# One-core cross-attention and SwiGLU kernel: float64 weights converted in pieces of 1024, exponent bounds on ScalarE, attention one batch ahead

## The chip, the core and the metric

The kernel runs on one NeuronCore of a Trainium2 chip. The engines are named as the profile names them: PE (TensorE, matmuls; PEld its weight loads), DVE (VectorE), ACT (ScalarE), POOL (GpSimd) and SP (SyncE, which here only issues DMAs). The metric is the device time of one execution in microseconds (us), lower is better. Each engine takes its instructions in the order in which the program has them and waits at an instruction until what that one needs is there.

## The reference

Inputs are float32 but for the three weight matrices, which arrive as float64: `x` [8, 8, 512, 64], `state` [8, 8, 32, 64], `w_gate` and `w_val` [512, 1536], `w_out` [1536, 512], `rms_g` [512].

```
# attention, for each batch and head
scores  = scale * x @ state.T;   a  = softmax(scores);   xread = a @ state     # 512 rows
scores2 = scale * state @ x.T;   a2 = softmax(scores2);  sread = a2 @ x        # 32 rows
x = concat(xread, sread), heads side by side           # 4352 rows of 512
# feed-forward
xn  = x / sqrt(mean(x * x) + 1e-6) * rms_g
g   = xn @ w_gate;  val = xn @ w_val
out = (g * sigmoid(g) * val) @ w_out
```

## The kernel before

For each of the 8 batches there are 512 token rows and 32 state rows. `attention(b)` is a generator: each `yield` ends a step, and the main program draws steps from it between other work. It transposes the state (`rows`, copied to `stT`), transposes `x` (`xT`, four copies out of PSUM, two by DVE and two by ACT), forms the scores, then first the state side (`e2` = exp, scaled on DVE by 1/sum, transposed into `e2T`, multiplied with `x` to `sr`), then the token side (`eS`, `aT`), the squares of the read-out (`ss`), their inverse root (`ri`), and spreads that along the free dimension: `along` multiplies the identity with it (`dg`, POOL) and PE multiplies `ones` with `dg`. What is left of a batch is `aT_s`, the scaled attention weights. `bd` is the state laid out block by block; DMAs write it.

Since a token's row is a mix of 32 state rows per head, the first feed-forward layer is applied to the state: `make_v` multiplies state and weights (`pv` in PSUM, `v` by ACT), and the hidden layer multiplies `v` with `aT_s`. Batch 0 does that plainly (`hidden`, then `project`). Batches 1 to 7 use a seven-product scheme for 2x2 blocks (`hidden_seven`, `project_seven`), which needs sums made beforehand: `slot_sums` of `aT_s`, `vs` of `v`, both on POOL, and `weight_sums` of `wo` on DVE, once. The state rows of all batches are normalised by `state_norm` and go last.

The weights: `pieces` lists 36 pieces of [128, 512], 12 each of gate, value and output. `load_piece` brings the 64-bit words into one of four `raw` buffers; `to_float32` takes them apart as two int32 halves: DVE shifts out the exponent (L152, `ex`), POOL bounds it and shifts it into place (L154, L155), ACT turns the low word to float32 (L156, `man`), DVE takes the mantissa's upper part (L157, `top`), adds the two (L158), puts the sign on (L160), and POOL multiplies both (L162) into `w` or `wo`. `ready(n)` converts up to piece n.

Order: a recording layer and its scheduler put the instructions on each engine's queue; the program's order gives the priorities. Attention runs two batches ahead (`LOOKAHEAD`): attentions 0 and 1 stand ahead of batch 0's hidden layer, with pieces converted between their steps, attention 2 beside it, and `project` behind all 36 pieces. In batch b, one step of attention b+2 follows each pair of hidden blocks, and up to four follow each of four places in `project_seven`. PSUM: `hidden`, `hidden_seven` and both projections share four banks (`fx` two, `fy`, `fz`), the attention has two (`at`), `pv` two.

Of the kernel before, what the change touches and what calls it, by code (L numbers as in the profile page):

```python
# [18 lines left out]
LOOKAHEAD = 2  # L19
# [3 lines left out]
def kernel(  # L23
# [37 lines left out]
    three = ctx.enter_context(tc.tile_pool(name="three", bufs=3))  # L61
# [17 lines left out]
    def load_state(b):  # L79

        rows[b] = two.tile([P, 2, D], F32, name="rows")
        for j in range(4):
            src = state[b, 2 * j:2 * j + 2].rearrange("e n d -> n e d")
            nc.sync.dma_start(out=rows[b][Ns * j:Ns * j + Ns], in_=src)
            nc.sync.dma_start(out=bds[b % 2][Ns * j:Ns * j + Ns, :, j, :], in_=src)
# [10 lines left out]
    load_state(0)  # L96
    load_x(0)
    rms_g = consts.tile([P, NI], F32, name="rms_g")
    nc.sync.dma_start(out=rms_g, in_=moe_rms_g.rearrange("(i p) -> p i", p=P))
# [3 lines left out]
    GE.memset(ones, 1.0)  # L103

# [4 lines left out]

    pieces = []  # L110
    for m in range(NM):
        for k, dram in enumerate((moe_w_gate, moe_w_val)):
            pieces.append((w[:, :, m, k, :],
                           dram[:, P * m:P * m + P].rearrange("(i p) f -> p i f", p=P)))
    for m in range(NM):
        pieces.append((wo[:, m].rearrange("p (i f) -> p i f", i=NI),
                       moe_w_out[P * m:P * m + P, :].rearrange("p (i f) -> p i f", i=NI)))
    raw = {}

    def load_piece(k):  # L120
# [3 lines left out]
        if src.dtype == F32:  # L124
            nc.sync.dma_start(out=dst, in_=src)
            return
        raw[k] = raws.tile([P, NI, 2 * P], I32, name="raw")
        nc.sync.dma_start(out=raw[k], in_=src.bitcast(I32))
# [10 lines left out]
    def to_float32(k):  # L139
# [6 lines left out]
        words = r.rearrange("p i (f two) -> p i f two", two=2)  # L146
        hi = words[:, :, :, 1]
        lo = r.bitcast(U32).rearrange("p i (f two) -> p i f two", two=2)[:, :, :, 0]
        top = conv.tile([P, NI, P], I32, name="top")
        ex = conv.tile([P, NI, P], I32, name="ex")  # L150
        man = conv.tile([P, NI, P], F32, name="man")
        VE.tensor_scalar(ex, hi, 20, 0x7ff, op0=ALU.logical_shift_right, op1=ALU.bitwise_and)  # L152

        GE.tensor_scalar(ex, ex, 1151.0, 896.0, op0=ALU.min, op1=ALU.max)  # L154
        GE.tensor_scalar(ex, ex, -896.0, float(1 << 23), op0=ALU.add, op1=ALU.mult)  # L155
        SE.activation(out=man, in_=lo, func=ACTF.Copy, scale=2.0 ** -52)  # L156
# [5 lines left out]
        GE.tensor_tensor(out=pieces[k][0], in0=man, in1=ex.bitcast(F32), op=ALU.mult)  # L162
# [13 lines left out]
    def along(ri, n):  # L176

        dg = one.tile([P, NC, P], F32, name="dg", tag="xT1")
        GE.tensor_tensor(out=dg[:, 0:n, :], in0=ident.unsqueeze(1).to_broadcast([P, n, P]),
# [6 lines left out]
    def attention(b):  # L186
        xb, bd = x_sb.pop(b), bds[b % 2]

        stT = two.tile([P, 4, Ns], F32, name="stT")
        stT_g[b] = three.tile([P, 4, Ns], F32, name="stT_g")  # L190
        tp = aps.tile([P, 4, Ns], F32, name="at")
        TE.transpose(out=tp.rearrange("p j n -> p (j n)"),
                     in_=rows.pop(b).rearrange("p e d -> p (e d)"), identity=ident)
        VE.tensor_copy(stT, tp)
        VE.tensor_tensor(out=stT_g[b], in0=stT, in1=rms_g.unsqueeze(2).to_broadcast([P, 4, Ns]),
# [4 lines left out]
        for j in range(4):  # L200
# [25 lines left out]
        GE.tensor_scalar(m2, m2, -SCALE, None, op0=ALU.mult)  # L226
# [3 lines left out]
        GE.tensor_scalar(z2, z2, 1e-9, None, op0=ALU.add)  # L230
# [6 lines left out]
        for e in range(2):  # L237
# [3 lines left out]
            VE.tensor_copy(e2T[:, e], tp)  # L241
# [11 lines left out]
        VE.tensor_copy(sr, rp.rearrange("p e d -> p (e d)"))  # L253
# [27 lines left out]
        GE.tensor_scalar(z, z, 1e-9, None, op0=ALU.add)  # L281
# [24 lines left out]
        if b + 2 < B:  # L306
# [340 lines left out]
```

## Time and profile before

| | |
|---|---|
| median of 3 runs | 948.27 us (945.02 to 948.87) |
| profiled execution | 948.93 us, its span 947.1 us |
| ACT, busy | 297.7 us (31%) |
| POOL, busy | 284.7 us (30%) |
| moved by DMA | 38.01 MB, of it 28.31 MB read |
| weight pieces | 36 DMAs of 512 KB, median 3.2 to 3.7 us to landing |

The page has one execution of the program. Its first part gives busy time by engine, its second cuts the span into 40 slices (a digit is tenths of busy time), its fourth follows the chain of work that ended last from the end back, its fifth groups instructions by line and operation: busy time and mean of one | idle time ahead of them and who ended it. "f<-aT_s,v" is an instruction that writes tile f and reads aT_s and v. A float32 matmul of the program stands as two matmul instructions in the trace.

### The profile page before, as it was taken

The page shows a single profiled execution, that of the slowest core. Times are in us where ns is not written, and L with a number is a line of the kernel's source. Part 1 is how long each engine was busy: PE and PEld are TensorE (multiplying, and loading weights), DVE is VectorE, ACT ScalarE, POOL GpSimd, SP SyncE. Part 2 cuts the span into 40 slices and gives each one's busy share as a digit, 9 for nine tenths or more (in the row PEclk, how much of TensorE's full clock was granted, in tenths as well). Part 3 has the DMA queues.
Part 4 walks back from the last instruction along what each step waited for, and adds up shares of the span by engine and source line. Part 5 has one row for each costly group of instructions (what it writes and reads, how often), then busy time and mean ns, then how long its engine had stood idle before and what let it go on. Part 6 is the DMA issues. An engine that isn't in the chain of part 4 may idle for free.

```text
span 947.1 us, 12086 instructions
## 1 busy us (share of the span) xinstructions
PE 863.2 (91%) x4726; PEld 623.0 (66%) x4726; DVE 508.8 (54%) x758; ACT 297.7 (31%) x550; POOL 284.7 (30%) x365
## 2 busy tenths in 40 slices
PE   3377668799999999999999999999998999999998
PEld 1133333344778867886778677867785778778886
DVE  4999987830475257525752575257523651571131
ACT  2234343300452245224522452145223520530110
POOL 3676675700323042303230333033303330320000
PEclk9557977899999999999999999999998999999999
DMA  6643524000002100200021002000000001000000
GB/s 185 160 135 115 156 98 142 17 11 23 15 1 45 34 18 1 46 34 18 1 45 34 15 1 46 34 12 1 1 34 12 1 1 41 5 1 23 23 1 23
DMA packets 62793, 38.01 MB, mean 40 GB/s; under 512 B 40720, under 2 KB 60688, under 8 KB 62736
## 3 DMA queue, kind: packets, MB, share of 16 engines
q1 hardware_dynamic: 62736, 37.24, 13.9%
q8 instruction: 37, 0.61, 0.3%
q14 instruction: 20, 0.16, 0.1%
HBM read 28.31 MB, written 8.91 MB: 39 GB/s over the span
## 4 chain that ended last, share of the span: by engine, by line
PE 80%; DVE 9%; POOL 7%; issue 3%; ACT 1%; DMA 1%; SPq 0%; POOLq 0%; DVEq 0%; ACTq 0%
PE f L487 29%; PE f L408 27%; PE pv L344 5%; PE f L370 5%; PE f L452 4%; PE at L301 2%; DVE man L158 2%; DVE top L157 2%; DVE ex L160 2%; PE at L182 1%; PE at L203 1%; POOL ex L154 1%; POOL ex L155 1%; DVE ex L152 1%; PE at L214 1%
## 5 line engine op out<-in xcount | busy, mean ns | idle before, releaser
L408 PE MATMUL f<-aT_s,v 128*128 128x256 f32 x504 | 131.6, 395 | 0.0
L408 PEld LDWEIGHTS f<-aT_s,v 128*128 128x128 f32 x504 | 89.5, 190 | 48.5 <-issue 30.6
L487 PE MATMUL f<-wo,hb 128*128 128x256 f32 x540 | 121.1, 380 | 0.0
L487 PEld LDWEIGHTS f<-wo,hb 128*128 128x128 f32 x540 | 101.6, 190 | 14.4 <-ACT ot L507 0.5
L359 POOL TENSOR_TENSOR vs<-v 128x256 f32<-128x256 f32 x42 | 31.3, 746 | 236.7 <-ACT v L351 236.7
L408 PE MATMUL f<-aT_t,vs 128*128 128x256 f32 x336 | 86.8, 381 | 0.0
L487 PE MATMUL f<-wt,hs 128*128 128x256 f32 x360 | 84.2, 385 | 0.0
L507 ACT COPY ot<-f 128x256 f32<-128x256 f32 x60 | 19.6, 375 | 194.7 <-PE f L487 194.7
L344 PE MATMUL pv<-w,stT_g 64*32 64x512 f32 x768 | 77.4, 641 | 2.2 <-POOL w L162 2.2
L487 PEld LDWEIGHTS f<-wt,hs 128*128 128x128 f32 x360 | 66.2, 190 | 15.7 <-PE at L214 4.2
L351 ACT COPY v<-pv 128x512 f32<-128x512 f32 x96 | 51.8, 590 | 73.3 <-PE pv L344 69.1
L408 PEld LDWEIGHTS f<-aT_t,vs 128*128 128x128 f32 x336 | 64.4, 192 | 8.9
L512 DVE TENSOR_TENSOR ot<-ot,f 128x256 f32<-128x256 f32 x45 | 17.0, 417 | 88.6 <-PE f L487 77.0
L370 PE MATMUL f<-aT_s,v 128*128 128x512 f32 x96 | 50.9, 668 | 9.3 <-DVE t L376 9.3
L433 ACT ACTIVATE hb<-g 128x1024 f32<-128x1024 f32 x42 | 44.4, 1057 | 44.9 <-DVE g L427 44.9
L434 DVE SCALAR_TENSOR_TENSOR hb<-hb,g 128x1024 f32<-128x1024 f32 x42 | 51.5, 1226 | 10.5 <-ACT hb L433 10.5
L423 DVE TENSOR_TENSOR g<-g,f 128x512 f32<-128x512 f32 x42 | 28.8, 686 | 47.8 <-PE f L408 34.8
L427 DVE TENSOR_TENSOR g<-g,f 128x512 f32<-128x512 f32 x42 | 28.9, 688 | 38.8 <-PE f L408 38.8
L156 ACT ACTIVATE man<-raw 128x512 f32<-128x512 uint32 x36 | 24.6, 682 | 74.4 <-POOL w L162 56.9
L408 PE MATMUL f<-aT_t,v 128*128 128x256 f32 x168 | 43.7, 383 | 0.0
L408 PE MATMUL f<-aT_s,vs 128*128 128x256 f32 x168 | 43.1, 379 | 0.0
L370 PE MATMUL f<-xsT,w 128*128 128x256 f32 x192 | 41.6, 379 | 0.0
(111 smaller groups left out, 1394.3 us busy)
## 6 DMA issues: line engine op xcount, KB each, us to landing
x_b<-in_x_dram SPq DMA_DIRECT2D x32, 256.0 KB, 4.7
out_dram<-ot SPq DMA_DIRECT2D x56, 128.0 KB, 1.7
raw<-in_moe_w_gate_dram SPq DMA_DIRECT2D x12, 512.0 KB, 3.6
raw<-in_moe_w_val_dram SPq DMA_DIRECT2D x12, 512.0 KB, 3.7
raw<-in_moe_w_out_dram SPq DMA_DIRECT2D x12, 512.0 KB, 3.2
out_dram<-ot SPq DMA_DIRECT2D x4, 256.0 KB, 2.0
rows<-in_state_dram SPq DMA_DIRECT2D x32, 16.0 KB, 1.8
bd<-in_state_dram SPq DMA_DIRECT2D x32, 16.0 KB, 1.8
```

The lines of the kernel that those rows point to most:

```text
L156: SE.activation(out=man, in_=lo, func=ACTF.Copy, scale=2.0 ** -52)
L344: TE.matmul(out=pv[e][Ns * j:Ns * j + Ns, :], lhsT=stT_g[b][D * e:D * e + D, j, :], rhs=w[D * e:D * e + D, j, 2 * mp:2 * mp + 2].rearrange ...
L351: SE.copy(v[:, e].rearrange("p m k f -> p (m k f)"), pv[e])
L359: GE.tensor_tensor(out=vs[:, 0], in0=a21, in1=a22, op=ALU.add)
L370: TE.matmul(out=ps[:, 0:n], lhsT=lhs(i, k), rhs=r, start=(i == 0), stop=(i == len(rhs) - 1))
L408: TE.matmul(out=ps[:, i, :], lhsT=lhs[:, i, :], rhs=rhs, start=(start and i == 0), stop=True, skip_group_check=True)
L423: VE.tensor_tensor(out=g[:, :, 0, :], in0=g[:, :, 0, :], in1=ys, op=ALU.add)
L427: VE.tensor_tensor(out=g[:, :, 1, :], in0=g[:, :, 1, :], in1=zs, op=ALU.add)
L433: SE.activation(out=h, in_=gate, func=ACTF.Tanh, scale=0.5)
L434: VE.scalar_tensor_tensor(out=h, in0=h, scalar=1.0, in1=gate, op0=ALU.add, op1=ALU.mult)
L452: TE.matmul(out=op, lhsT=hb[:, m, P * r:P * r + P], rhs=wo[:, m, :], start=(m == 0), stop=(m == NM - 1))
L487: TE.matmul(out=ps[:, r, :], lhsT=lhs(k)[:, P * r:P * r + P], rhs=rhs(k), start=(start and r == 0 and k == 0), stop=(k == HM - 1), skip_gr ...
```

## The change

- **Pieces of 1024.** 18 pieces instead of 36, each of [128, 1024] (two blocks of 128 columns of gate or value, or two row blocks of `wo`). `man` is no tile of its own any more: it is written over the low words in the `raw` buffer.
- **Exponent bounds on ACT.** The two POOL operations L154 and L155 become two Relus of ACT (L153 and L154 of the changed kernel), with biases from a new tile `bounds`.
- **Copies and small operations.** ACT makes all copies of `xT` and `e2T`. `e2` is no longer scaled by 1/sum on DVE; the scaling is in the copy to `sr`. `dg` and some operations on small tiles go from POOL to DVE. `bd` is copied out of `rows` by POOL, four copies per batch, in place of four DMAs.
- **One attention ahead.** Attention b+1 runs in batch b; batch 0's hidden layer has no attention's steps beside it. Two steps follow each pair of hidden blocks, and `slot_sums` and the first `make_v` of the next batch (`prepare`) stand ahead of the last two of `project_seven`'s products.
- **Batch 0's projection.** All four row blocks are accumulated at once, block m of `wo` after block m, so that it can take `wo` piece by piece; attention 1's steps stand between.
- **Start.** Weight piece 0 is loaded ahead of `x`, and `rms_g` behind the first four pieces.

The diff, cut to its core:

```diff
-    for m in range(NM):
+    for mp in range(NM // 2):
         for k, dram in enumerate((moe_w_gate, moe_w_val)):
-            pieces.append((w[:, :, m, k, :],
+            pieces.append((w[:, :, 2 * mp:2 * mp + 2, k, :],
...
-        raw[k] = raws.tile([P, NI, 2 * P], I32, name="raw")
+        raw[k] = raws.tile([P, 8 * P, 2], I32, name="raw")
...
+        hi = r[:, :, 1]
+        man = r.bitcast(F32)[:, :, 0]
+        top = conv.tile([P, 8 * P], I32, name="top")
+        ex = conv.tile([P, 8 * P], I32, name="ex")
...
-        GE.tensor_scalar(ex, ex, 1151.0, 896.0, op0=ALU.min, op1=ALU.max)
-        GE.tensor_scalar(ex, ex, -896.0, float(1 << 23), op0=ALU.add, op1=ALU.mult)
-        SE.activation(out=man, in_=lo, func=ACTF.Copy, scale=2.0 ** -52)
+        SE.activation(out=ex, in_=ex, func=ACTF.Relu, scale=-1.0, bias=bounds[:, 0:1])
+        SE.activation(out=ex, in_=ex, func=ACTF.Relu, scale=-float(1 << 23), bias=bounds[:, 1:2])
+        SE.activation(out=man, in_=r.bitcast(U32)[:, :, 0], func=ACTF.Copy, scale=2.0 ** -52)
...
-        GE.tensor_tensor(out=dg[:, 0:n, :], in0=ident.unsqueeze(1).to_broadcast([P, n, P]),
+        VE.tensor_tensor(out=dg[:, 0:n, :], in0=ident.unsqueeze(1).to_broadcast([P, n, P]),
...
+        for j in range(4):
+            GE.tensor_copy(bd[Ns * j:Ns * j + Ns, :, j, :], packed[Ns * j:Ns * j + Ns])
...
-            if j % 2:
-                SE.copy(xT[j // 2][:, j % 2], tp)
-            else:
-                VE.tensor_copy(xT[j // 2][:, j % 2], tp)
+            SE.copy(xT[j // 2][:, j % 2], tp)
...
-        for e in range(2):
-            VE.tensor_scalar(e2[:, e], e2[:, e], z2[:, e:e + 1], None, op0=ALU.mult)
...
-            VE.tensor_copy(e2T[:, e], tp)
+            SE.copy(e2T[:, e], tp)
...
-        VE.tensor_copy(sr, rp.rearrange("p e d -> p (e d)"))
+        for e in range(2):
+            VE.tensor_scalar(sr[:, D * e:D * e + D], rp[:, e, :], z2[:, e:e + 1], None,
+                             op0=ALU.mult)
...
-    def project(n, store, between):
-        for r in range(n // P):
-            op = (fx, fy, fz, fx)[r].tile([P, DM], F32, name="f")
-            for m in range(NM):
+    def project_as_ready(store, between):
+        banks = [f.tile([P, DM], F32, name="f") for f in (fx, fy, fz, fx)]
+        for m in range(NM):
+            if m % 2 == 0:
+                ready(NM + m // 2 + 1)
+                between(m)
+            for r, op in enumerate(banks):
                 TE.matmul(out=op, lhsT=hb[:, m, P * r:P * r + P], rhs=wo[:, m, :],
                           start=(m == 0), stop=(m == NM - 1))
...
+    def prepare(b):
+        if b < B:
+            slot_sums(b)
+            make_v(b, 0)
...
+    load_state(0)
+    load_piece(0)
+    load_x(0)
+    for k in range(1, RAW_AHEAD):
         load_piece(k)
-    load_state(1)
-    for k, _ in enumerate(attention(0)):
-        if k % 2:
-            ready(n_ready + 1)
+    nc.sync.dma_start(out=rms_g, in_=moe_rms_g.rearrange("(i p) -> p i", p=P))
+    for _ in attention(0):
+        pass
     make_v(0, 0)
-    for k, _ in enumerate(attention(1)):
-        if k % 2:
-            ready(n_ready + 1)
...
-        if b + LOOKAHEAD < B:
-            steps = attention(b + LOOKAHEAD)
+        steps = attention(b + 1) if b + 1 < B else state_norm()
...
-                between()
-            slot_sums(b + 1)
-            make_v(b + 1, 0)
-            ready(len(pieces))
-            early.close()
-            project(S, store_tokens(b), between)
+            def between(m):
+                some(5)
+                if m == NM - 4:
+                    ready(len(pieces))
+                    early.close()
+                    open_late()
+                    some(20)
+                    prepare(b + 1)
+            project_as_ready(store_tokens(b), between)
...
-                next(steps, done)
+                some(2)
                 next(sums, done)
-            project_seven(S, store_tokens(b), lambda: (between(), between()))
+            project_seven(S, store_tokens(b), lambda: some(5), lambda: prepare(b + 1))
```

How the instructions now stand, at three places. First PE where batch 0's projection begins. Before, it reads (L370 is the hidden layer, L182 `along` of attention 2, L452 the projection, L408 batch 1's first products):

```order
L370 MATMUL f<-aT_s,v 128x512 x2
L182 MATMUL at<-dg,ones 128x512
L370 MATMUL f<-aT_s,v 128x512 x6
L452 MATMUL f<-wo,hb 128x512 x48
L408 MATMUL f<-aT_s,v 128x256 x2
L408 MATMUL f<-aT_t,vs 128x256 x2
```

In the change, the second half of attention 1 (L272, L294, L304, L184) stands inside the projection (L457), and batch 1's first `make_v` (L345) too:

```order
L272 MATMUL at<-ident,sS 128x128 x8
L457 MATMUL f<-wo,hb 128x512 x8
L294 MATMUL at<-ident,eS 128x128 x8
L457 MATMUL f<-wo,hb 128x512
L304 MATMUL at<-bd_86,aT 128x256 x8
L457 MATMUL f<-wo,hb 128x512 x2
L184 MATMUL at<-dg,ones 128x512
L457 MATMUL f<-wo,hb 128x512 x5
L345 MATMUL pv<-w,stT_g 32x512 x8
L457 MATMUL f<-wo,hb 128x512 x16
L409 MATMUL f<-aT_s,v 128x256 x2
```

No projection matmul has moved ahead of the last hidden one; 48 matmuls in one row have become pieces of 1 to 16 with attention 1 between them.

Second PE at the end of a later batch, where the next attention's scaling is made. Before, at the end of batch 1, for attention 3 (L301 its read-outs, L487 the projection, L182 `along`, L344 `make_v`):

```order
L301 MATMUL at<-bd_89,aT 128x256 x5
L487 MATMUL f<-wo,hs 128x256 x11
L487 MATMUL f<-wt,hb 128x256 x12
L301 MATMUL at<-bd_89,aT 128x256 x2
L408 MATMUL f<-aT_s,v 128x256 x2
L408 MATMUL f<-aT_t,vs 128x256 x2
L182 MATMUL at<-dg,ones 128x512
L344 MATMUL pv<-w,stT_g 32x512 x8
```

In the change, the same place for attention 2, which batch 2 needs next (L304, L500, L184, L345 in the same roles):

```order
L304 MATMUL at<-bd_85,aT 128x256 x4
L500 MATMUL f<-wo,hb 128x256 x4
L184 MATMUL at<-dg,ones 128x512
L500 MATMUL f<-wo,hb 128x256 x20
L345 MATMUL pv<-w,stT_g 32x512 x8
L500 MATMUL f<-wo,hs 128x256 x12
L500 MATMUL f<-wt,hb 128x256 x12
L409 MATMUL f<-aT_s,v 128x256 x2
L409 MATMUL f<-aT_t,vs 128x256 x2
```

`along` now comes 44 projection matmuls ahead of the batch's end instead of after it, with four matmuls between it and the last read-outs, as before.

Third DVE in batch 0's hidden layer. Before (L152, L157, L158 and L160 convert, L376 and L378 are the hidden layer's):

```order
L152 TENSOR_SCALAR ex<-raw 128x512
L157 TENSOR_SCALAR top<-raw 128x512
L376 SCALAR_TENSOR_TENSOR t<-t,f 128x512
L158 SCALAR_TENSOR_TENSOR man<-top,man 128x512
L160 SCALAR_TENSOR_TENSOR ex<-raw,ex 128x512
L378 SCALAR_TENSOR_TENSOR hb<-t,f 128x512
```

And in the change (L151, L156, L157, L159 convert, L377 and L379 are the hidden layer's):

```order
L159 SCALAR_TENSOR_TENSOR ex<-raw,ex 128x1024
L377 SCALAR_TENSOR_TENSOR t<-t,f 128x512
L151 TENSOR_SCALAR ex<-raw 128x1024
L379 SCALAR_TENSOR_TENSOR hb<-t,f 128x512
L157 SCALAR_TENSOR_TENSOR raw<-top,raw 128x1024
L151 TENSOR_SCALAR ex<-raw 128x1024
L156 TENSOR_SCALAR top<-raw 128x1024
L377 SCALAR_TENSOR_TENSOR t<-t,f 128x512
L159 SCALAR_TENSOR_TENSOR ex<-raw,ex 128x1024
L379 SCALAR_TENSOR_TENSOR hb<-t,f 128x512
```

The converting operations are twice as long and half as many, and no attention's operations stand between them any more. In the whole program, ahead of the first `aT_s`, 13 of 36 pieces had their sign put on before and 7 of 18 have now; the last of them stands right ahead of the last `hb`.

More of the change, by code (lines that the diff above doesn't have):

```diff
@@ L103 @@
     GE.memset(ones, 1.0)
+    bounds = consts.tile([P, 2], F32, name="bounds")
+    GE.memset(bounds[:, 0:1], 1151.0)
+    GE.memset(bounds[:, 1:2], 255.0 * (1 << 23))
+    rms_g = consts.tile([P, NI], F32, name="rms_g")
     w = consts.tile([P, NI, NM, 2, P], F32, name="w")
@@ L305, in attention @@
             yield
-        if b + 2 < B:
-            load_state(b + 2)
         rp = along(inverse_rms(ss, NC), NC)
-        aT_s[b] = three.tile([P, 2, S], F32, name="aT_s")
+        aT_s[b] = two.tile([P, 2, S], F32, name="aT_s")
         VE.tensor_tensor(out=aT_s[b], in0=aT.rearrange("p e c t -> p e (c t)"),
@@ L353, in make_v @@
         if b in aT_t:
-            vs = two.tile([P, 3, 2, P], F32, name="vs")
+            vs = seven["vs"].tile([P, 3, 2, P], F32, name="vs")
             v_sb[b, mp] = v, vs
```

83 lines of the change are left out of this document (36 added, 47 removed).

## The prediction

> **What bounds the kernel now.** I read the page's first two parts first, to see whether one limit holds for the whole span.
>
> ```profile
> PE 863.2 (91%) x4726; PEld 623.0 (66%) x4726; DVE 508.8 (54%) x758; ACT 297.7 (31%) x550; POOL 284.7 (30%) x365
> PE   3377668799999999999999999999998999999998
> DVE  4999987830475257525752575257523651571131
> ```
>
> It does not. PE is full from the ninth slice on (a slice is 23.7 us) and half idle before it, and there DVE is full. So I cut the span with the view of windows, and took the chain of work that ended last for the place where the limit changes.
>
> ```profile
> 14.40:73.40 59.00, 30.91 (x174) 12.94 (x172) 54.98 (x76) 19.23 (x37) 43.52 (x47) 0.60 0.52 150
> 73.40:184.20 110.80, 82.20 (x432) 37.95 (x427) 98.59 (x149) 41.10 (x81) 75.19 (x82) 0.85 0.38 112
> 335.80:432.70 96.90, 95.27 (x592) 73.74 (x593) 50.56 (x74) 35.46 (x66) 24.16 (x34) 1.00 0.09 24
> 806.00:887.00 81.00, 81.00 (x412) 65.57 (x413) 38.09 (x54) 24.06 (x41) 14.16 (x20) 1.00 0.04 14
> ```
>
> ```profile
> 197.79 41.20 PE f L452 x96
> 238.99 1.73 PE f L408 x8
> ```
>
> In a window's row stand PE, PEld, DVE, ACT and POOL, then the granted clock. From 14.4 to 184.2 us DVE is busy 54.98 + 98.59 = 153.6 of 169.8 us, a share of 0.904; ACT only 60.3. This is the **conversion stage**: float64 weights to float32, beside attentions 0, 1 and 2 and batch 0's hidden layer. Batch 0's projection (L452) then runs from 197.79 to 238.99 and batches 1 to 7 from 238.99 to the end, with PE as the limit. I therefore ask three things: when does the first projection matmul come (P, now 197.8), how long is it from P to batch 1's first product (now 41.2), and what changes in the 708.1 us behind that.
>
> **First term: the conversion stage.** These groups, from the view of lines for that window (DVE's costliest, then POOL's), are what the change cuts.
>
> ```profile
> L160 DVE SCALAR_TENSOR_TENSOR ex<-raw,ex 128x512 int32<-128x512 int32 x36 | 32.4, 901 | 5.0 <-POOL ex L155 5.0
> L158 DVE SCALAR_TENSOR_TENSOR man<-top,man 128x512 f32<-128x512 int32 x36 | 31.6, 878 | 0.3
> L157 DVE TENSOR_SCALAR top<-raw 128x512 int32<-128x512 int32 x36 | 29.0, 808 | 0.0
> L152 DVE TENSOR_SCALAR ex<-raw 128x512 int32<-128x512 int32 x36 | 22.4, 621 | 0.0
> L378 DVE SCALAR_TENSOR_TENSOR hb<-t,f 128x512 f32<-128x512 f32 x10 | 6.7, 677 | 0.0
> L376 DVE SCALAR_TENSOR_TENSOR t<-t,f 128x512 f32<-128x512 f32 x10 | 6.7, 676 | 0.0
> ```
>
> ```profile
> L162 POOL TENSOR_TENSOR w<-man,ex 128x512 f32<-128x512 f32 x24 | 33.1, 1378 | 22.1 <-DVE ex L160 16.3 <-DVE man L158 5.6
> L154 POOL TENSOR_SCALAR ex<-ex 128x512 int32<-128x512 int32 x36 | 28.4, 789 | 19.9 <-DVE ex L152 18.1
> L155 POOL TENSOR_SCALAR ex<-ex 128x512 int32<-128x512 int32 x36 | 28.2, 784 | 2.9
> L162 POOL TENSOR_TENSOR wo<-man,ex 128x512 f32<-128x512 f32 x12 | 15.9, 1321 | 15.1 <-DVE ex L160 13.9 <-DVE man L158 1.2
> L173 POOL TENSOR_TENSOR ri<-ss,mhalf 128x4 f32<-128x4 f32 x2 | 2.7, 1345 | 0.0
> L179 POOL TENSOR_TENSOR dg<-ident,ri 128x512 f32<-128x512 f32 x2 | 2.2, 1078 | 0.2
> ```
>
> They can be much shorter, as the view of one tile has it (least, median, longest in ns), and two stretches of the timeline show why.
>
> ```profile
> L157 DVE TENSOR_SCALAR top<-raw x36: 414/828/1550, 14.8 to 178.8; 128x512 int32<-128x512 int32 x36
> ```
>
> ```profile
> 48.94 1.39 POOL L162 TENSOR_TENSOR w<-man,ex 128x512 f32<-128x512 f32 x1 [2.36 <-DVE ex L160]
> ...
> 49.11 1.51 DVE L157 TENSOR_SCALAR top<-raw 128x512 int32<-128x512 int32 x1
> ...
> 181.85 1.27 DVE L376 SCALAR_TENSOR_TENSOR t<-t,f 128x512 f32<-128x512 f32 x2
> 182.01 1.29 POOL L162 TENSOR_TENSOR wo<-man,ex 128x512 f32<-128x512 f32 x1 [1.23 <-DVE man L158]
> ```
>
> A POOL product runs to 50.33; the DVE operation beside it ends at 50.62, 1.1 us longer than its best of 0.41. So **DVE stands still while POOL works on SBUF**. L376, which reads PSUM, does not: two in 1.27 us under a product. In all, DVE's four lines are busy 32.4 + 31.6 + 29.0 + 22.4 = 115.4 us; not held up, with 0.41 for L152 and L157 and L376's 0.68 for the other two, they would take 36 x (2 x 0.41 + 2 x 0.68) = 78.5. The other 36.9 us are such waits, 35% of POOL's 33.1 + 15.9 + 28.4 + 28.2 = 105.6.
>
> The change makes 18 pieces of 1024 out of 36 of 512, and its two Relus on ACT take the place of L154 and L155. Rows of 1024 stand on the page:
>
> ```profile
> L433 ACT ACTIVATE hb<-g 128x1024 f32<-128x1024 f32 x42 | 44.4, 1057 | 44.9 <-DVE g L427 44.9
> L434 DVE SCALAR_TENSOR_TENSOR hb<-hb,g 128x1024 f32<-128x1024 f32 x42 | 51.5, 1226 | 10.5 <-ACT hb L433 10.5
> ```
>
> DVE per piece: 2 x 0.82 (twice L157's best; nothing taken off for a shared start) + 2 x 1.23 = 4.1 us, in 18 pieces 74 us. The hidden layer's 12 x (0.676 + 0.677) is 16.2. Attention 0: a batch with an attention has 50.56 us of DVE and one without 38.09, so 12.5 each; the change takes six operations of about 0.6 off (two xT copies, two e2T copies, two scalings of e2) and puts dg and some tiny ones on: 10. Sum 100 us. The waits: only the products are left on POOL, 49 us if a product of 1024 costs twice one of 512, and 35% of that is 17. Sum 117; at the old busy share 117 / 0.904 = 129 us.
>
> When it starts:
>
> ```profile
> 8.71 0.51 SPq L128 DMA_DIRECT2D raw<-in_moe_w_gate_dram  x1
> ```
>
> ```profile
> 14.42 0.42 DVE L152 TENSOR_SCALAR ex<-raw 128x512 int32<-128x512 int32 x1
> ```
>
> The first piece is now issued behind eight state DMAs, four of x and one of rms_g; in the change behind four state DMAs, about 2.9 us. With the same 5.7 us to its first use that is 8.6. So **P = 8.6 + 129 = 138**. Bounds: with no waits and no idle DVE 8.6 + 100 = 109; with DVE standing still under every product (100 + 49) / 0.904 + 8.6 = 173. I take 138 because the share of 35% is measured on this pair of engines; the mix of operations differs, hence both ends stay.
>
> ACT: 18 x 2 Relus at 1.06 = 38 us more, plus four copies (two of xT, two of e2T) that an attention moves from DVE. 60.3 + 38 less two attentions that leave the stage: at most 98 of 129 us, so it is hidden by DVE's own work. What the trace doesn't show is a Relu on int32, in and out; below it is a copy's price, above it, as a bound, a product's price on POOL, 2 x 1.38; 1.06 is nearest, being the same engine and size. If that cover is gone, see the second rival. The product now reads man at every second word, which no row shows for POOL: below, nothing (DVE reads raw so in 0.41); above, twice, 98 us, still under DVE's 129; I take nothing. DMAs: the pieces move the same bytes; their buffers are freed by the product as before; state is read once, not twice, and POOL's four small copies of it lie beside PE work.
>
> A rule of the Trainium skill bears on the waits: "SBUF — State Buffer", section "Who interferes with whom", has the port pair that VectorE and GpSimd share as an exclusive lock, held for the whole instruction, against VectorE operations in a two-port mode or with two SBUF inputs. The trace agrees at 49.11 (1.51 us, to 0.29 behind the product's end) and at L376 (one input in PSUM, no wait). Taken for every product the rule gives P = 173, taken at the measured share 138.
>
> **Second term: projection and attention 1.** Before, attentions 1 and 2 are done when the projection starts. In the changed order no projection matmul stands ahead of the last hidden matmul: their PSUM banks are the hidden layer's, and the last conversion stands just ahead of the last hb on DVE. So taking wo piece by piece starts nothing early; it only lets attention 1 fill in. An attention's PE time:
>
> ```profile
> 430.84 1.02 PE pv L344 x16
> ...
> 525.90 1.02 PE pv L344 x16
> ...
> 803.18 1.73 PE f L408 x8
> ...
> 882.87 41.44 PE f L370 x192
> ```
>
> ```profile
> 714.71 1.13 PE L182 MATMUL at<-dg,ones 128*128 128x512 f32 x2 [1.63 <-POOL dg L179]
> ```
>
> A batch with attention takes 525.90 - 430.84 = 95.06 us, the last one without 79.69. The difference of 15.4 holds 1.0 of pv for a next batch and 1.6 of waiting for dg, so 12.7 are the attention. From P: 41.2 + 12.7 + 1.0 (batch 1's pv now stands here) + 4.5 of stalls, which are an estimate: 1.3 at dg, and some 3 where e, e2T, aT and the squares have one or two matmuls of 0.86 for cover. That is 59.4 (56 to 68), so batch 1's first product comes at 138 + 59.4 = 197.4 instead of 239.0: 41.6 us earlier.
>
> **Third term: batches 1 to 7.** Attention 2 now lies here: +12.7 + 1.6. The wait for dg shrinks from 1.6 to about 1.3, since dg moves to DVE (0.68 for an operation of 512, 1.08 on POOL) behind the same 1.7 us of matmuls: -2 in six batches. New places without cover (scores right behind the last copy of xT, e2T's reader right behind its transposes): 6 x 0.5 = +3. The weight sums leave batch 1, which took 96.8 us, not 95.1: -1.7. Sum **+13.5** (+8 to +30). The slot sums behind aT_s (four POOL operations of 256, at most 1.4 each, like a product) have 44 matmuls of 256 as cover, 0.43 each, half of 41.20 / 48: 19 us.
>
> **Sum.** Against this execution, whose span is 947.1 and whole time 948.9: 947.1 - 41.6 + 13.5 = 919.0, with 1.8 around it 920.8; the median of the runs stands 0.7 under it, so 920. In short, time = P + 782.
>
> **Rivals.**
> First, slower: DVE loses the whole of every product. Place: SBUF operations of DVE queued right behind each ex that releases a product; price 49 us instead of 17; P = 173, time 955. It decides from about 42 us of waits on (P = 166). For it speaks 49.11; against it the 35%, and that the order often puts a hidden-layer operation on PSUM, which doesn't wait, behind ex. 0.06. The Trainium skill's "SBUF — State Buffer" ("Who interferes with whom") states this as the rule.
> Second, the longer chain of a piece: 0.82 + 2 x 1.06 + 1.23 + 2.7 and some 0.4 of hand-overs, 7.3 us, where ACT is in order and its tanh waits for PE. If pieces then go one at a time, 18 x 7.3 = 131, with the hidden layer's 16 P = 156, time 938. Two ex buffers and four raw ones speak against it. 0.10.
> Third, the one attention ahead becomes late in every batch: PE waits for eS or aT. From 4.5 us in each of six batches the gain is gone; time 943 to 950. The 80 us of other PE work per batch speak against it. 0.05.
> Fourth, better: DVE waits little and PE sets the pace. Attention 0, now done where the first window ends, at 73.4, comes 5.8 us earlier like the first piece, near 68; the hidden layer's 48 matmuls have the projection's shape and number, so 41 us; five pv groups 5 to 8: P = 114 to 117, time 898. Against it: a PE with a granted clock of 0.60 and 0.85 in this stage. 0.14.
>
> **How the numbers follow.** My forecast, 905 to 935, has 0.65. The range reaches to the fourth and the second rival: 896 to 942. More than 0.5% (some 4.7 us, about what a measurement of this kernel can tell from no change) faster: 0.65 + 0.14 + 0.10 = 0.89; within it 0.05; slower 0.06.
>
> **What would show it.** Right: first projection matmul near 138; DVE's conversion lines near 91 us in sum (74 + 17), with bests of 0.8 and 1.2 us; Relu near 1.06; batch 1's first product near 197; later batches 94 to 96 us. Wrong: P near 115 or 160; ACT idle under 10% in the stage; DVE waiting for ACT's Relus; a batch over 98 us, with PE waiting for eS, aT or dg.

## The result, and the profile after

| | before | after |
|---|---|---|
| median of the runs | 947.12 us (945.02 to 948.87) | 911.82 us (910.17 to 914.00) |
| span of the profiled execution | 947.1 us | 911.7 us |
| start of batch 0's run of projection matmuls (P) | 197.6 us | 133.5 us |
| batch 1's first product | 238.8 us | 188.4 us |
| from there to the end of the span | 708.3 us | 723.3 us |

The ratio is 0.963, 95% interval 0.9595 to 0.9665: faster, by 35 us. The forecast was 920. In the changed kernel one projection matmul (two instructions in the trace) stands alone at 127.9 us, and the run itself starts at 133.5; P is the start of the run in all that follows. The page's first two parts after the change:

```profile
PE 845.7 (93%) x4726; PEld 621.0 (68%) x4726; DVE 474.2 (52%) x679; ACT 346.7 (38%) x600; POOL 212.0 (23%) x276
PE   3559779999999999999999999999999999999997
DVE  4899996036822583167415761476246822571131
```

PE is now full from the seventh slice on, not the ninth. Cut where the limit changes (columns: PE, PEld, DVE, ACT, POOL, granted clock), the view of windows has:

```profile
8.00:60.00 52.00, 29.84 (x185) 14.57 (x185) 43.82 (x50) 38.01 (x52) 20.47 (x12) 0.87 0.74 220
60.00:133.50 73.50, 57.24 (x165) 23.20 (x166) 72.25 (x68) 43.55 (x54) 32.44 (x17) 0.88 0.35 116
133.50:188.40 54.90, 53.00 (x235) 25.20 (x235) 17.84 (x31) 11.54 (x26) 10.21 (x15) 0.97 0.11 24
285.77:381.27 95.50, 93.23 (x573) 73.25 (x573) 47.30 (x72) 36.54 (x68) 22.19 (x34) 1.00 0.09 24
```

DVE still bounds the conversion stage: 43.82 + 72.25 = 116.1 of 125.5 us, a share of 0.925. The next row is batch 0's projection with attention 1 in it, and there PE is busy for 53.0 of 54.9 us. The last is one later batch. What DVE, POOL and ACT do for the conversion, from the view of lines for the first 200 us:

```profile
L157 DVE SCALAR_TENSOR_TENSOR raw<-top,raw 128x1024 f32<-128x1024 int32 x18 | 26.0, 1443 | 1.2 <-ACT raw L155 0.8
L159 DVE SCALAR_TENSOR_TENSOR ex<-raw,ex 128x1024 int32<-128x1024 int32 x18 | 25.8, 1435 | 1.6 <-ACT ex L154 1.6
L151 DVE TENSOR_SCALAR ex<-raw 128x1024 int32<-128x1024 int32 x18 | 22.5, 1248 | 10.6 <-DMA raw<-in_moe_w_gate_dram 7.8 <-DMA raw<-in_moe_w_val_dram 2.8
L156 DVE TENSOR_SCALAR top<-raw 128x1024 int32<-128x1024 int32 x18 | 16.3, 908 | 0.0
```

```profile
L162 POOL TENSOR_TENSOR w<-raw,ex 128x1024 f32<-128x1024 f32 x12 | 30.7, 2557 | 49.0 <-DVE ex L159 45.0 <-issue 3.9
L162 POOL TENSOR_TENSOR wo<-raw,ex 128x1024 f32<-128x1024 f32 x6 | 15.4, 2566 | 22.7 <-DVE ex L159 22.7
```

```profile
L154 ACT ACTIVATE ex<-ex,bounds 128x1024 int32<-128x1024 int32 x18 | 20.8, 1155 | 0.2
L153 ACT ACTIVATE ex<-ex,bounds 128x1024 int32<-128x1024 int32 x18 | 20.6, 1147 | 27.7 <-DVE ex L151 27.7
```

DVE's four lines sum to 90.6 us (115.4 before). Two lines of one kind differ, 1248 against 908 ns: L151 overlaps a product on POOL in seven of its 18 pieces, L156 in five. The two Relus lie on ACT without making DVE wait for more than 1.6 us in all (L159's idle time).

### The profile page after: what moved, and what is told of

It is laid out like the page before. It is cut to its first block, busy times and chain, and to the rows that moved or that the text cites. A ratio compares the mean times of both kernels' runs of the same rounds, so it can differ in the third digit from the quotient of the medians.

```text
span 911.7 us, 11827 instructions
## 1 busy us (share of the span) xinstructions
PE 845.7 (93%) x4726; PEld 621.0 (68%) x4726; DVE 474.2 (52%) x679; ACT 346.7 (38%) x600; POOL 212.0 (23%) x276
## 4 chain that ended last, share of the span: by engine, by line
PE 66%; issue 16%; DVE 8%; ACT 4%; POOL 3%; DMA 1%; SPq 1%; ACTq 0%; DVEq 0%; POOLq 0%
PE f L500 22%; PE f L409 22%; PE pv L345 5%; PE f L371 5%; PE f L457 4%; PE at L304 2%; PE at L217 2%; PE at L209 2%; DVE ex L151 1%; PE at L184 1%; POOL ri L175 1%; DVE ex L159 1%; ACT e L231 1%; DVE dg L181 1%; DVE m L226 1%
## 5 line engine op out<-in xcount | busy, mean ns | idle before, releaser
L409 PEld LDWEIGHTS f<-aT_s,v 128*128 128x128 f32 x504 | 89.1, 190 | 51.5 <-issue 30.6
L500 PE MATMUL f<-wo,hb 128*128 128x256 f32 x540 | 121.6, 379 | 0.0
L500 PEld LDWEIGHTS f<-wo,hb 128*128 128x128 f32 x540 | 102.5, 190 | 16.7 <-issue 2.9
L500 PE MATMUL f<-wt,hs 128*128 128x256 f32 x360 | 83.5, 382 | 0.0
L500 PEld LDWEIGHTS f<-wt,hs 128*128 128x128 f32 x360 | 67.7, 190 | 10.3 <-DVE g L428 0.3
L345 PE MATMUL pv<-w,stT_g 64*32 64x512 f32 x768 | 65.7, 616 | 3.4 <-DVE z L233 1.9
L371 PE MATMUL f<-aT_s,v 128*128 128x512 f32 x96 | 48.6, 662 | 9.1 <-DVE t L377 7.6
L200 POOL COPY bd<-rows 32x128 f32<-32x128 f32 x32 | 13.5, 423 | 150.5 <-PE at L304 148.8
L371 PEld LDWEIGHTS f<-aT_s,v 128*128 128x128 f32 x96 | 19.4, 211 | 38.7 <-issue 19.7
L542 DVE TENSOR_TENSOR hs<-hb,hs 128x768 f32<-128x768 f32 x15 | 14.4, 959 | 59.5 <-PE f L500 59.5
L457 PE MATMUL f<-wo,hb 128*128 128x512 f32 x96 | 44.7, 612 | 0.0
```

The lines of the kernel that those rows point to most:

```text
L345: TE.matmul(out=pv[e][Ns * j:Ns * j + Ns, :], lhsT=stT_g[b][D * e:D * e + D, j, :], rhs=w[D * e:D * e + D, j, 2 * mp:2 * mp + 2].rearrange ...
L371: TE.matmul(out=ps[:, 0:n], lhsT=lhs(i, k), rhs=r, start=(i == 0), stop=(i == len(rhs) - 1))
L409: TE.matmul(out=ps[:, i, :], lhsT=lhs[:, i, :], rhs=rhs, start=(start and i == 0), stop=True, skip_group_check=True)
L457: TE.matmul(out=op, lhsT=hb[:, m, P * r:P * r + P], rhs=wo[:, m, :], start=(m == 0), stop=(m == NM - 1))
L500: TE.matmul(out=ps[:, r, :], lhsT=lhs(k)[:, P * r:P * r + P], rhs=rhs(k), start=(start and r == 0 and k == 0), stop=(k == HM - 1), skip_gr ...
```

## The experiments

Theory: the conversion stage got shorter mainly because DVE loses a share of all that POOL does in SBUF, and the bounds left POOL. Rivals: the size of the pieces, the place of the attention, wo taken piece by piece, or the copies moved to ACT made the gain. In the diffs "-" is the kernel named at the head, "+" the experiment. All runs stand against the kernel before on the same chip, whose median was 947.1 to 949.1 us over these series, so that a difference of about 2 us between two experiments carries no weight.

**Undoing parts of the changed kernel (911.8 us).** The bounds back on POOL:

```diff
-SE.activation(out=ex, in_=ex, func=ACTF.Relu, scale=-1.0, bias=bounds[:, 0:1])
-SE.activation(out=ex, in_=ex, func=ACTF.Relu, scale=-float(1 << 23), bias=bounds[:, 1:2])
+GE.tensor_scalar(ex, ex, 1151.0, 896.0, op0=ALU.min, op1=ALU.max)
+GE.tensor_scalar(ex, ex, -896.0, float(1 << 23), op0=ALU.add, op1=ALU.mult)
```

> The changed kernel with the two exponent bounds back on POOL, on its pieces of 1024. Theory (DVE loses a share of whatever POOL does in SBUF): POOL gets 18 x 2 operations of about 1.57 us (twice the 0.79 of 512) = 57 us, of which DVE loses 35 to 48% = 20 to 27 us; at the old busy share 22 to 30 us later, so about 934 to 942 us. Rival (the size of the pieces and the attention's place made the gain, and where the bounds stand does not matter, since POOL is idle half of that stage): 910 to 917 us.

Measured: 928.4 us, ratio 0.979 (0.977 to 0.982), 16.5 us more than the changed kernel. That is between the two, nearer to the theory. DVE's four lines and POOL's, in the view of lines:

```profile
L157 DVE SCALAR_TENSOR_TENSOR raw<-top,raw 128x1024 f32<-128x1024 int32 x18 | 31.1, 1730 | 1.0 <-ACT raw L155 0.5
L159 DVE SCALAR_TENSOR_TENSOR ex<-raw,ex 128x1024 int32<-128x1024 int32 x18 | 29.6, 1646 | 2.8 <-POOL ex L154 2.8
L156 DVE TENSOR_SCALAR top<-raw 128x1024 int32<-128x1024 int32 x18 | 27.4, 1525 | 0.0
L151 DVE TENSOR_SCALAR ex<-raw 128x1024 int32<-128x1024 int32 x18 | 22.6, 1258 | 9.9 <-DMA raw<-in_moe_w_gate_dram 7.9 <-DMA raw<-in_moe_w_val_dram 2.0
```

```profile
L162 POOL TENSOR_TENSOR w<-raw,ex 128x1024 f32<-128x1024 f32 x12 | 32.4, 2698 | 14.8 <-DVE ex L159 9.7 <-DVE z L284 3.4 <-DVE m L229 1.6
L154 POOL TENSOR_SCALAR ex<-ex 128x1024 int32<-128x1024 int32 x18 | 29.5, 1638 | 1.5
L153 POOL TENSOR_SCALAR ex<-ex 128x1024 int32<-128x1024 int32 x18 | 25.6, 1422 | 11.3 <-DVE ex L151 10.5
L162 POOL TENSOR_TENSOR wo<-raw,ex 128x1024 f32<-128x1024 f32 x6 | 14.9, 2486 | 10.6 <-DVE ex L159 7.7 <-DVE raw L157 2.9
```

DVE's lines do not change what they compute, yet sum to 110.7 us instead of 90.6; P comes 16 us later (149.5). The 20 us of waits were expected, but not that DVE's busy share rises with them (133.5 of 141.5 us, 0.944), which took back a part.

The product on DVE:

```diff
-GE.tensor_tensor(out=dst, in0=man..., in1=ex..., op=ALU.mult)
+VE.tensor_tensor(out=dst, in0=man..., in1=ex..., op=ALU.mult)
```

> The changed kernel with the product man x ex on DVE. Theory (waits on POOL's product are about 22 us in the changed kernel's conversion): DVE gets 18 x 1.23 = 22 us of work and loses about 22 us of waits, so about the same: 906 to 918 us; L151 and L156 then keep near their best of 0.69 us in all 18 pieces. Rival (the long DVE operations beside a product are cover that costs nothing, DVE's own work sets the pace): 22 / 0.9 = 24 us longer, 936 us.

Measured: 890.4 us, ratio 0.939 (0.936 to 0.941): 21 us faster than the changed kernel, below both. The view of lines:

```profile
L159 DVE SCALAR_TENSOR_TENSOR ex<-raw,ex 128x1024 int32<-128x1024 int32 x18 | 21.9, 1224 | 1.9 <-ACT ex L154 1.8
L157 DVE SCALAR_TENSOR_TENSOR raw<-top,raw 128x1024 f32<-128x1024 int32 x18 | 21.9, 1218 | 0.9 <-ACT raw L155 0.8
L162 DVE TENSOR_TENSOR w<-raw,ex 128x1024 f32<-128x1024 f32 x12 | 14.7, 1224 | 0.0
L151 DVE TENSOR_SCALAR ex<-raw 128x1024 int32<-128x1024 int32 x18 | 12.3, 686 | 9.4 <-DMA raw<-in_moe_w_gate_dram 7.9 <-DMA raw<-in_moe_w_val_dram 1.5
L156 DVE TENSOR_SCALAR top<-raw 128x1024 int32<-128x1024 int32 x18 | 12.3, 691 | 0.0
L162 DVE TENSOR_TENSOR wo<-raw,ex 128x1024 f32<-128x1024 f32 x6 | 7.2, 1220 | 0.0
```

The four old lines now take 21.9 + 21.9 + 12.3 + 12.3 = 68.4 us, their time without any wait, and the product 21.9: 90.3 in all, against 90.6. The exchange is even on DVE, as the theory had it, and yet 21 us are gained. Two things could make them. The product is a step of 1.2 us instead of 2.4 us on another engine; and the order on DVE changed, for four pieces of wo now stand behind the last hb, where in the changed kernel all 18 stand ahead of it. The latter was tried by itself, and the former by adding a POOL product that nobody waits for.

Four pieces of wo behind the last hb, in the changed kernel:

```diff
-top = conv.tile([P, 8 * P], I32, name="top")
-ex = conv.tile([P, 8 * P], I32, name="ex")
+late = k >= len(pieces) - 4
+top = (two if late else conv).tile([P, 8 * P], I32, name="top", tag="g" if late else "top")
+ex = (two if late else conv).tile([P, 8 * P], I32, name="ex", tag="g" if late else "ex")
```

> The changed kernel, product still on POOL, but the last four pieces of wo take their two integer tiles from the pool of the hidden layer's t, so that their DVE operations can't stand ahead of the last hb any more (in the changed kernel all 18 pieces stand ahead of it, in product_on_dve only 14). Theory (what product_on_dve gained beyond an even exchange is these four pieces, some 20 us of DVE work that went behind the first projection matmul and lies beside PE there): first projection matmul at 112 to 118 us, 893 to 902 us in all. Rival (its gain was the end of DVE's standing still alone, the place of wo's last pieces does not matter): 907 to 915 us.

Measured: 907.9 us, ratio 0.957 (0.955 to 0.959). P moved, if less far than the theory said, to 121.0, but batch 1's first product only from 188.4 to 183.8: the rival's time. The windows show why.

```profile
60.00:120.90 60.90, 52.70 (x155) 21.52 (x156) 50.74 (x54) 35.30 (x45) 23.28 (x12) 0.89 0.42 140
120.90:183.80 62.90, 55.74 (x247) 27.27 (x245) 31.80 (x46) 20.10 (x35) 18.10 (x18) 0.95 0.09 21
```

With wo's pieces gone from before P, neither PE nor DVE is full there; behind P, PE idles 7.2 us, where it idled 1.9: 5.3 us for ACT's `e` of attention 1 and 1.9 for dg. An earlier P alone is worth little. The edit also brings a wait of its own, since the late pieces share two buffers: `top` (L157 in this run) waits 4.8 us for POOL's product. So it does not price the order cleanly.

A POOL product that nobody waits for, added to product_on_dve:

```diff
 VE.tensor_tensor(out=dst, in0=man..., in1=ex..., op=ALU.mult)
+GE.tensor_tensor(out=ex.bitcast(F32), in0=man, in1=ex.bitcast(F32), op=ALU.mult)
```

> product_on_dve (890.4 us) with one more POOL product per piece that nobody waits for: the same two inputs as the product on DVE, written over ex. Theory (DVE stands still beside POOL's work in SBUF): 18 x 2.4 = 43 us of POOL, of which DVE loses 48% = 21 us, 23 us later in all: 908 to 916 us, like the changed kernel. Rival (product_on_dve gained because 1.2 us on DVE is a shorter step of a piece's chain than 2.4 us on POOL and a hand-over, and because four pieces of wo come behind the last hb): 889 to 896 us.

Measured: 915.2 us, ratio 0.965 (0.962 to 0.968): all of the gain is gone again. From the view of lines:

```profile
L157 DVE SCALAR_TENSOR_TENSOR raw<-top,raw 128x1024 f32<-128x1024 int32 x18 | 29.3, 1626 | 0.1
L156 DVE TENSOR_SCALAR top<-raw 128x1024 int32<-128x1024 int32 x18 | 22.4, 1251 | 0.0
L159 DVE SCALAR_TENSOR_TENSOR ex<-raw,ex 128x1024 int32<-128x1024 int32 x18 | 22.1, 1228 | 1.6 <-ACT ex L154 1.6
L151 DVE TENSOR_SCALAR ex<-raw 128x1024 int32<-128x1024 int32 x18 | 20.0, 1111 | 11.8 <-DMA raw<-in_moe_w_gate_dram 8.0 <-POOL ex L165 2.3 <-DMA raw<-in_moe_w_val_dram 1.5
```

```profile
L165 POOL TENSOR_TENSOR ex<-raw,ex 128x1024 f32<-128x1024 f32 x18 | 49.1, 2729 | 89.4 <-DVE w L162 52.4 <-DVE wo L162 17.2 <-issue 13.5
```

The four lines are back at 93.8 us, 25.4 over 68.4. DVE waited directly for the added product (for the buffer of ex) only 2.3 us. L159, which in this order stands just ahead of the products, keeps its best time; the lines behind them lose. So **what a POOL product costs this stage is DVE's standing still**, 25 us of it here, and not a longer chain. Nothing waits for the added result; what stands behind it on POOL could come late too, but DVE's wait for POOL's `ri` up to batch 1 was 6.6 us, against 7.6 without the added product.

How the 21 us that product_on_dve gained divide is not settled. DVE's sum is the same as in the changed kernel (90.3 against 90.6 us), so the end of the waits paid for the product there and no more; besides, four pieces, some 20 us of DVE by this sum, now lie beside PE's work behind P, and that order alone, with the product still on POOL, gave 3.9 us (wo_late). PE was quicker as well: its 584 instructions from 8 us to batch 1's first product were busy 132.1 us at a mean granted clock of 0.93, against 140.1 us at 0.91 in the changed kernel. Whether the clock rose because PE waited less is not shown.

**The other parts, undone.**

```diff
-SE.copy(xT[j // 2][:, j % 2], tp)
+if j % 2:
+    SE.copy(xT[j // 2][:, j % 2], tp)
+else:
+    VE.tensor_copy(xT[j // 2][:, j % 2], tp)
...
-SE.copy(e2T[:, e], tp)
+VE.tensor_copy(e2T[:, e], tp)
```

> The changed kernel with half of xT's copies and both of e2T's back on DVE. Theory (neither engine is the limit in batches 1 to 7, and in the conversion one attention costs DVE 4 x 0.6 = 2.4 us): 911 to 916 us. Rival (ACT's copies are what PE waits for in the attentions, part of the 15 us that batches 1 to 7 gained in length): 903 to 908 us.

Measured: 912.3 us, ratio 0.9615 (0.959 to 0.964). The copies' place changes nothing.

Projection by rows (the new code's core):

```diff
-for m in range(NM):
-    if m % 2 == 0:
-        ready(NM + m // 2 + 1)
-        between(m)
-    for r, op in enumerate(banks):
+ready(len(pieces))
...
+for r, f in enumerate((fx, fy, fz, fx)):
+    op = f.tile([P, DM], F32, name="f")
+    for m in range(NM):
+        if m % 4 == 0:
+            between(3 * r + m // 4)
```

> The changed kernel with batch 0's projection row block by row block again (all of wo converted first), attention 1 between its matmuls in twelve places. Theory (wo piece by piece starts nothing early, since the banks come free only with the last hidden matmul, and the last piece is converted by then): 909 to 918 us. Rival (taking wo as it becomes ready is part of the gain): batch 0's projection waits for the last of wo, 920 us or more.

Measured: 908.6 us, ratio 0.957 (0.955 to 0.959), 3.3 us less than the changed kernel and just under the theory's span. Taking wo piece by piece is not part of the gain; it costs a little. Its four read-outs come all at the end, through two buffers that batch 1's g needs next. The chain of the changed kernel (start, duration, what):

```profile
186.02 0.59 ACT ot L461
...
186.63 2.05 DMA out_dram<-ot
...
188.78 0.59 ACT ot L461
...
189.40 3.63 DMA out_dram<-ot
...
193.10 0.59 ACT g L419
```

Batch 1's first g waits for the stores until 193.10, 4.7 us behind its first product (188.40); by rows the same g comes 1.1 us behind it (186.38 after 185.27).

**Parts alone, on the kernel before.** Relus only (bounds_only):

```diff
-GE.tensor_scalar(ex, ex, 1151.0, 896.0, op0=ALU.min, op1=ALU.max)
-GE.tensor_scalar(ex, ex, -896.0, float(1 << 23), op0=ALU.add, op1=ALU.mult)
+SE.activation(out=ex, in_=ex, func=ACTF.Relu, scale=-1.0, bias=bounds[:, 0:1])
+SE.activation(out=ex, in_=ex, func=ACTF.Relu, scale=-float(1 << 23), bias=bounds[:, 1:2])
```

> The kernel before with nothing but the exponent bounds moved from POOL to two Relus on ACT, in its 36 pieces of 512. Theory (DVE loses about a third of what POOL does in SBUF; 56.6 us leave POOL): 20 us of waits less, 22 at the old busy share: 924 to 932 us. Rival (POOL's idle time hides the bounds, gain from pieces and order): 944 to 950 us.

Measured: 925.5 us, ratio 0.976 (0.973 to 0.978): two lines of code (and the tile with their biases) give 23.6 of the change's 35 us.

Pieces of 1024 only (pieces_only; it takes the diff's lists of pieces and its DVE, ACT and POOL product lines, POOL bounds kept):

```diff
-RAW_AHEAD = 4
+RAW_AHEAD = 3
...
-top = conv.tile([P, NI, P], I32, name="top")
-ex = conv.tile([P, NI, P], I32, name="ex")
-man = conv.tile([P, NI, P], F32, name="man")
+man = r.bitcast(F32)[:, :, 0]
+top = conv.tile([P, 8 * P], I32, name="top")
+ex = conv.tile([P, 8 * P], I32, name="ex")
```

> The kernel before with pieces of 1024 (three ahead instead of four of half the size, for room), bounds still on POOL, attention still two ahead. Theory (fixed cost of 36 x 4 operations halves: best times 0.41 and 0.68 at 512, 0.69 and 1.22 at 1024, so 18 x 2 x (0.13 + 0.14) = 10 us off DVE): 936 to 942 us. Rival (the longer chain of a piece over three engines shows): 948 to 960 us.

Measured: 944.8 us, ratio 0.996 (0.995 to 0.998), between the two. DVE's four lines fell to 26.8 + 24.9 + 24.3 + 18.6 = 94.6 us, 21 less than before, yet P came at 196.7 instead of 197.6: the sum of these lines does not set P by itself. DVE was busy 155 of 182 us instead of 161 of 183, 6 us less and not 21, since other operations grew longer (`e<-e,z` took 1.69 us in the mean, 0.93 before) or came earlier. The edit also does more than its name says: it converts at every fourth step of an attention instead of every second, and it puts batch 1's slot sums and first `make_v` behind the last piece. On POOL the four slot sums, which ran from 124.7 us on before, now come between 179.0 and 184.4, ahead of ss, ri and dg of attention 2, and PE waits for that dg right ahead of P:

```profile
190.72 2.07 PE L186 MATMUL at<-dg,ones 128*128 128x512 f32 x2 [4.30 <-POOL dg L183]
```

What pieces of 1024 are worth without this is not shown.

Both, with attention still two ahead and the projection by rows (conversion_only):

```diff
 (the lines of pieces_only, and)
-GE.tensor_scalar(ex, ex, 1151.0, 896.0, op0=ALU.min, op1=ALU.max)
-GE.tensor_scalar(ex, ex, -896.0, float(1 << 23), op0=ALU.add, op1=ALU.mult)
+SE.activation(out=ex, in_=ex, func=ACTF.Relu, scale=-1.0, bias=bounds[:, 0:1])
+SE.activation(out=ex, in_=ex, func=ACTF.Relu, scale=-float(1 << 23), bias=bounds[:, 1:2])
```

> The kernel before with the whole new conversion (pieces of 1024, three ahead, bounds on ACT), but attention two ahead and the projection by rows as before. Theory (the attention's move gives back in batches 1 to 7 about what it takes from the conversion stage): 905 to 916 us, like the changed kernel. Rival (the attentions' move is a good part of the gain): 922 to 932 us.

Measured: 924.4 us, ratio 0.9745 (0.973 to 0.976): the rival's time. PE's rows in the timeline:

```profile
174.46 41.36 PE L459 MATMUL f<-wo,hb 128*128 128x512 f32 x96
215.66 1.03 PE L415 MATMUL f<-aT_s,v 128*128 128x256 f32 x4
```

Batch 1's first product comes at 215.7 and 706.7 us follow; in the changed kernel 188.4 and 723.3. So what the change does beside the conversion wins 27.3 us ahead of that point and gives 16.6 back behind it, 11 to 12 us in all. The attentions' move was not tried alone: the copies, dg, bd, the projection's order and the start are in this sum too (the copies and the projection's order gained nothing, as their runs above show). Some of it is also the slot sums again, which this edit too puts ahead of attention 2's ss on POOL. PE waits longer for dg than the 3.9 us of the kernel before:

```profile
167.29 2.07 PE L189 MATMUL at<-dg,ones 128*128 128x512 f32 x2 [6.82 <-POOL dg L186]
```

The new conversion as a whole gives 24.7 us here, and the bounds alone gave 23.6. Whether the pieces of 1024 add to that stays open because of this wait.

**Can it be faster?** PE waits for dg 1.9 us in each attention, and the timeline of the changed kernel shows what stands ahead of it:

```profile
260.04 0.58 ACT L307 ACTIVATE at<-at 128x512 f32<-128x512 f32 x1 [0.28 <-PE at L304]
260.88 1.33 POOL L200 COPY bd<-rows 32x128 f32<-32x128 f32 x4 [29.98 <-PE at L304]
260.91 0.58 ACT L307 ACTIVATE at<-at 128x512 f32<-128x512 f32 x1 [0.17 <-PE at L304]
262.29 0.19 POOL L173 TENSOR_SCALAR ss<-ss 128x4 f32<-128x4 f32 x1
262.57 1.02 POOL L175 TENSOR_TENSOR ri<-ss,mhalf 128x4 f32<-128x4 f32 x1
263.62 0.69 DVE L181 TENSOR_TENSOR dg<-ident,ri 128x512 f32<-128x512 f32 x1 [3.54 <-POOL ri L175]
264.46 1.10 PE L184 MATMUL at<-dg,ones 128*128 128x512 f32 x2 [1.93 <-DVE dg L181]
```

The four copies into bd, for a later attention, are released by the same matmuls as the squares, and stand on POOL ahead of ss.

```diff
-GE.tensor_copy(bd[Ns * j:Ns * j + Ns, :, j, :], packed[Ns * j:Ns * j + Ns])
+VE.tensor_copy(bd[Ns * j:Ns * j + Ns, :, j, :], packed[Ns * j:Ns * j + Ns])
```

> product_on_dve (890.4 us) with the four small copies of the state into bd on DVE instead of POOL, so that they stand no longer ahead of ss on POOL. Theory (the 1.9 us that PE waits for dg in each batch hold these 1.3 us): 7 attentions x 1.3 = 9 us less, 880 to 884 us, and PE's wait for dg at 0.3 to 0.6 us. Rival (the wait is the chain ss, ri, dg itself, and the copies now stand ahead of dg on DVE): 888 to 892 us.

Measured: 884.3 us, ratio 0.933 (0.930 to 0.9355), 6.1 less than product_on_dve, between the two. The waits of PE for dg from 240 us on (in all, times, longest), product_on_dve and then product_bd:

```profile
PE at L184 <- DVE dg L181: 11.1, 7, 1.9
```

```profile
PE at L184 <- DVE dg L181: 7.6, 6, 1.6
```

In the later batches 1.93 us become 1.31 (a batch takes 94.9 instead of 95.5 us): ss, ri and dg are a chain of their own, 2.2 us from ss on, so the copies' 1.3 us are only half won.

Projection by rows on top of product_on_dve (the diff of projection_by_rows):

> product_on_dve (890.4 us) with batch 0's projection row block by row block. There four pieces of wo are converted behind the last hb, so that taking wo piece by piece could matter, as it did not in the changed kernel (projection_by_rows 908.6 against 911.8 us). Theory: the first row block waits for the last piece, the rest is not hidden, 898 to 906 us. Rival (attention 1 sets when the projection ends, in either order): 886 to 892 us.

Measured: 887.7 us, ratio 0.936 (0.932 to 0.939): 2.7 us faster, the rival. Even with four pieces converted behind the last hb, rows cost nothing.

All three together:

> All three edits that were faster, together: product on DVE, bd's copies on DVE, batch 0's projection by rows. Theory (the rows move batch 0 alone, bd's copies the six batches behind it, so the gains add): 890.4 - 6.1 - 2.7 = 881.6, so 880 to 883 us. Rival (both shorten the same end of attention 1 in batch 0's projection): 883 to 886 us.

Measured: 881.9 us, ratio 0.931 (0.928 to 0.934), as the theory added them: 30 us under the changed kernel.

## Why the prediction was right

**First term, P.** Forecast 138, measured 133.5 (the first single matmul, which the forecast's words name, came at 127.9, but the sum of DVE's work describes the start of the run). Its parts held: DVE's conversion lines 90.6 us (91), all DVE work 116.1 (117), Relus 1.15 us (1.06), the start 8.0 (8.6), the product of 1024 2.56 us (2.7). The waits were taken too low and the work too high, and the two cancelled: 22.2 us of waits (90.6 - 68.4) instead of 17, since DVE lost 48% of POOL's 46.1 us and not 35%, and 68.4 of work instead of 74. The rest is the busy share, 0.925 instead of 0.904. ACT was hidden, but not behind the last piece, as the chain of waits of the changed kernel has it just ahead of P:

```profile
126.59 2.46 DVE ex L151
...
129.07 1.15 ACT ex L153
130.22 0.48 ACT t L376
130.70 1.04 ACT ex L154
```

The last tanh stands between the two Relus of wo's last piece, so here the longer chain of a piece cost some 2 us once (an estimate, from the two Relus' 1.15 and 1.04 us), not 18 times.

The mechanism on which the term rests is shown in both directions: 102.4 us of POOL (29.5 + 25.6 and the products' 32.4 + 14.9 in bounds_on_pool) hold DVE up for 42.3 us, 49.1 (shadow_product) for 25.4, none (product_on_dve) for none. The first rival, the whole of every product lost, did not come: DVE spends part of a product's time on operations that do not wait or on none at all. Its decision point was wrong too: at 42 us of waits P was to be 166; bounds_on_pool has 42.3 and P at 149.5. The share of 0.904 is no constant: it is 0.944 there and 0.853 in pieces_only (155 of 182 us).

**Second term.** From P to batch 1's first product 54.9 us instead of 59.4. Of the 4.5 us that are missing, 2.6 are the estimate of 4.5 us of stalls: PE idled 1.9. The other 1.9 are work: PE was busy 53.0 us and not 54.9, since 15 of the 16 instructions of attention 1's transposes of x and one projection matmul ran ahead of P. Counted from that first matmul (127.9) the term would be 60.5, so how the miss divides between the first two terms depends on the mark; that batch 1's first product came at 188.4 instead of 197.4 does not. That no projection matmul comes ahead of the last hb was right but for two instructions of 96; that taking wo piece by piece starts nothing early held, and projection_by_rows shows that it costs 3 us, which the prediction did not see.

**Third term.** +13.5 forecast, 723.3 - 708.3 = +15.0 measured. Two of its steps were wrong. The wait for dg was to shrink from 1.6 to 1.3 us and grew to 1.9: the copies into bd, which the change moved to POOL, were counted as lying "beside PE work", and what stood behind them on POOL was not asked. The weight sums were to take 1.7 us off batch 1, but that reading took two different marks: 96.8 us run from batch 1's first product to the `make_v` behind batch 2's first products. From first product to first product batch 1 took 92.3 us before (238.8 to 331.1) and the next ones 95.1, so there was nothing to take off. In the changed kernel it took 97.2 us (188.4 to 285.6), of which the read-outs of the projection, which hold its first g up, are 1.7: with the projection by rows it takes 95.5. What was taken for places without cover (+3) was less: in a later batch PE is busy 93.23 of 95.50 us, and 1.9 of the rest is dg.

**The rivals.** The longer chain of a piece showed only there, and the late attention not at all: DVE waited for ACT's Relus 1.6 us, and PE in the later batches for little but dg. PE as the pace of the stage, the fourth, came true only once POOL was empty: in product_on_dve the window from 60 to 106 us, with PE in the first column, reads

```profile
60.00:106.00 46.00, 44.95 (x164) 18.51 (x163) 45.04 (x57) 33.00 (x41) 0.00 (x0) 1.00 0.51 174
```

with PE and DVE both full; the first projection matmul comes at 106.0, the run at 108.8. The forecast was thus right in its main cause, and 8 us off by its sizes: -4.5 in P, -4.5 behind it and +1.5 in the batches.

## What to carry to other kernels

Where DVE bounds a stage, count POOL's SBUF time there as DVE time, at a quarter to a half by these runs, even where nobody waits for its result; an operation that POOL needs 2.4 us for and DVE 1.2 is then better on DVE itself. Ask of every step that moves to an engine with little work what is queued behind it there: four copies of 0.3 us on an idle POOL cost PE 0.6 us in each batch. A shorter early stage counts only as far as the next stage's own supply (here wo, the attention) keeps up.

## What the runs showed of the hardware that was not expected

The share of POOL's time that DVE loses is no constant: (DVE's four lines less their time without waits) over POOL's time for the conversion was 36.9 of 105.6 us before, 22.2 of 46.1 after, 42.3 of 102.4 with the bounds on POOL, 25.4 of 49.1 under the added product and 26.2 of 95.9 in pieces_only, 27 to 52%. (In pieces_only other DVE operations were stretched, which this sum leaves out.) The Trainium skill, "SBUF — State Buffer", section "Who interferes with whom", has an exclusive lock in which the order of issue decides who waits; the runs agree: POOL's product too is stretched, from 2.40 us at its best to 2.56 in the mean and 2.73 for the added one, and L159 loses nothing where it stands ahead of the products (1.23 us in the mean) but 0.2 us where it may stand beside them (1.44). A product with an input at every second word took POOL 2.40 us for 1024 at its best, no more than twice the 1.26 that 512 without the stride took at its best before: the stride cost nothing that shows.
